# Moving the second pair's turn, the third pair's key loads and the sixth pair's loads in a fused attention and MLP kernel

## The chip, the cores and the metric

The kernel runs on one core of one Trainium2 chip. The metric is the device time of one execution in microseconds (us); lower is better. A core has a matrix engine (TensorE, in profiles PE, with its weight loads as PEld), a vector engine (VectorE, DVE), an activation engine (ScalarE, ACT), a general engine (GpSimd, POOL) and a sync engine (SyncE, SP) which here only issues DMAs. Each engine works through its own instructions in program order. Waits between engines go by semaphores. DMAs are issued by SP, ACT or POOL and run on 16 shared DMA engines.

## The reference

Attention with a threshold, over 8 batches of 8 heads with 576 rows of 64, then an MLP with exact GELU on the 4608 x 512 result.

```python
scores = scale * np.matmul(q, k.transpose(0, 1, 3, 2))
thresh = np.max(scores, axis=-1, keepdims=True) - tau
scores = np.where(scores >= thresh, scores, -1000000000.0)
scores = scores - np.max(scores, axis=-1, keepdims=True)
attn = np.exp(scores)
attn = attn / (np.sum(attn, axis=-1, keepdims=True) + 1e-09)
attn = np.matmul(attn, v).astype(np.float32)
...
h = x @ w_in                                            # 512 -> 2048
g = 0.5 * h * (1.0 + erf(h * inv_sqrt2))
return (g @ w_out).astype(np.float32)                   # 2048 -> 512
```

The MLP weights come in 64-bit floats, everything else in 32-bit floats.

## The kernel before

Heads are taken two at a time: a **pair** p holds two heads, 32 pairs in all, four to a batch. The 576 rows of a pair are four chunks of 128 and a tail of 64, so a pair has five pieces of work, one for each chunk i. One pass of the main loop is a **slot** (counted from 0): it computes the scores of one chunk of one pair on PE (`scores`, L366), their negated maxima on DVE (L378), thresholds on POOL (L379), exponentials on ACT (L381), and the thresholding with row sums on DVE (L397). Then DVE, POOL and ACT make two diagonal matrices of inverse sums (`diagonal`, L408, L411). In the next slot PE transposes the weights against these diagonals (`turn_p_early`, L308), and ACT copies them out of PSUM (L316, L320, L327). Later `weigh_v` multiplies them with the values (L483).

The first four pairs (p = 0 to 3) are the early ones. Their order is written out by hand: slots 0 to 7 take chunks 0 and 1 of pairs 0, 1, 2, 3 (slot 0 is pair 0 chunk 0, slot 1 is pair 0 chunk 1, slot 2 is pair 1 chunk 0, slot 4 is pair 2 chunk 0), slots 8 to 19 the other chunks of the four. `BATCH` is 20, the number of these slots. So slot 17 is chunk 2 of pair 3 and slot 18 its chunk 3.

`load_early` brings queries and keys of an early pair with rows on partitions: two DMAs for the main part and one for the tail, for queries (L248, L252) and for keys (L251, L252). `turn_qk_early` transposes both on PE (16 matmuls for queries, 16 for keys, L279; 8 small ones for the tails, L289), and copies them out of PSUM with five instructions: scaled queries on ACT (L282), keys (L284), two small copies of the key tail (L291, L292), and scaled query tails (two activations, L295). For pair 0 the key copies run on DVE, for the others on ACT. The pairs from 4 on are loaded by `load` in another layout, with runs of 128 bytes (L224 for q and k, L233 for v, after a small fill of the value tile by POOL, L228), and turned by DVE.

While the early pairs run, the weights are brought in 32 pieces of 512 columns, each by two DMAs (raw and shifted bytes, L155 and L157), and made 32-bit on DVE and ACT (L177, L178, L183, L185, L187). `load_piece` issues the next piece's DMAs once a piece has been used up: the first two from SP, the others from POOL. The buffers hold four pieces. `convert` places this work between the softmax steps of a slot. `fill` puts matmuls of the MLP (L558, L572) between the attention's wherever the weights are there. The last five blocks of 512 tokens are done after the attention with a scheme of seven products (L692).

The order of issue on each engine is that of the program. On SP it is: queries of pairs 0, 1, 2 (and what else `load_early` gives it), the first two weight pieces, values of pair 0, pair 3, values of pairs 1, 2, 3, then pair 4 and pair 5. SP has nothing else to do, so it comes to these long before the slot in whose text they stand, unless a buffer holds it up.

The piece of the main loop that the change touches:

```python
        if p < NP:
            scores(p, i)
            softmax_head(p, i)
            if p < HP - 1 and i == (1 if p == 0 else 0):
                turn_qk_early(p + 1)
```

Of the kernel before, what the change touches and what calls it, by code (L numbers as in the profile page):

```python
# [18 lines left out]
def kernel(  # L19
# [28 lines left out]
    nc = tc.nc  # L48
    ctx.enter_context(tc.manual_schedule())

    B, H, S, D = q.shape
    d_model, d_ff = moe_w_in.shape
    P = 128
    Q = 32
    HP = H // 2
# [4 lines left out]
    TAIL = S - MAIN  # L60
# [150 lines left out]
    def load(p):  # L211
        for _ in load_steps(p):
            pass
# [23 lines left out]
    def load_early(p):  # L237
        b, hp = divmod(p, HP)
        s = st[p] = {}
        for name, src in (("q", q), ("k", k)):  # L240

            pool, tag = (xg, "x") if p == 2 else (ld, name)
            t = s[name] = pool.tile([P, 2, NC + 1, D], FP32, tag=tag, name=name)
            eng = (nc.scalar, nc.gpsimd, nc.scalar)[p] if p < 3 and name == "k" else nc.sync
            for e in range(2):
                rows = src[b, 2 * hp + e, 0:MAIN, :]
                if name == "q":
                    eng.dma_start(t[:, e, 0:NC, :].rearrange("p (g c) d -> p g (c d)", c=2),  # L248
                                  rows.rearrange("(g p c) d -> p g (c d)", p=P, c=2))
                else:  # L250
                    eng.dma_start(t[:, e, 0:NC, :], rows.rearrange("(p t) d -> p t d", p=P))  # L251
            eng.dma_start(t[0:TAIL, :, NC, :], src[b, 2 * hp:2 * hp + 2, MAIN:S, :].rearrange("e s d -> s e d"))  # L252
# [8 lines left out]
    def turn_qk_early(p):  # L261


        s = st[p]
        if 2 <= p < HP:
            qT = op.tile([P, MAIN], FP32, tag="o_sb", name="qT")
            kT = pd_tail[p - 2].rearrange("p b i -> p (b i)")
        else:
            qT = ld.tile([P, MAIN], FP32, tag="qT", name="qT")
            kT = ld.tile([P, TAIL + S], FP32, tag="kT", name="kT")  # L270
        s["qT"], s["kT"] = qT, kT
        qt = s["q_tail"] = q_tail[p % 4]
        copy = nc.scalar.copy if p else nc.vector.tensor_copy
        for name in "qk":
            t = s[name]
            tr = ps.tile([P, NC, P], FP32, tag="mm", name="tr")
            for c in range(NC):
                for e in range(2):
                    nc.tensor.matmul(tr[e * D:(e + 1) * D, c, :], lhsT=t[:, e, c, :], rhs=ident, start=True, stop=True)  # L279
            src = tr.rearrange("p c s -> p (c s)")  # L280
            if name == "q":
                nc.scalar.activation(qT, src, AF.Copy, bias=0.0, scale=q_scale)  # L282
            else:
                copy(kT[:, TAIL:S], src)  # L284
        tr = ps.tile([P, NC, P], FP32, tag="mm", name="tr")
        for j, name in enumerate("qk"):
            t = s.pop(name)
            for e in range(2):
                nc.tensor.matmul(tr[e * D:(e + 1) * D, j, 0:TAIL], lhsT=t[0:TAIL, e, NC, :],  # L289
                                 rhs=ident[0:TAIL, 0:TAIL], start=True, stop=True)  # L290
        copy(kT[:, S:S + TAIL], tr[:, 1, 0:TAIL])  # L291
        copy(kT[D:P, 0:TAIL], tr[D:P, 1, 0:TAIL])  # L292
        for e in range(2):
            rows = slice(e * D, (e + 1) * D)
            nc.scalar.activation(  # L295
                qt[rows, e * TAIL:(e + 1) * TAIL], tr[rows, 0, 0:TAIL], AF.Copy, bias=0.0, scale=q_scale[rows])
# [60 lines left out]
    def scores(p, i):  # L357
        s = st[p]
        n = 1 if i == NC else 2
        sc = s["sc", i] = [ps.tile([P, 2, 512], FP32, tag="sc", name="sc", bufs=2) for _ in range(n)]  # L360
        for h in range(2):
            for e in range(n):
                rows = slice(0, P) if i == NC else slice(e * D, (e + 1) * D)
                lhsT = s["q_tail"] if i == NC else s["qT"][rows, i * P:(i + 1) * P]
                at = h * HALF + (TAIL if p < EARLY and e == 0 else 0)
                nc.tensor.matmul(  # L366
                    sc[e][:, h, 0:HALF], lhsT=lhsT, rhs=s["kT"][rows, at:at + HALF], start=True, stop=True)
# [150 lines left out]
    def gelus(left):  # L518


        while len(late) > left:
            g, j, hT = late.pop(0)
            t = gp.tile([P, 2, TOK], FP32, tag="g", name="g")
            if hold[0]:
                nc.scalar.copy(t, hT)
                held.append((g, j, t))
            else:
                gelu(g, j, t, hT)
# [6 lines left out]
    def gelus_held():  # L535
        hold[0] = False
        while held:
            g, j, t = held.pop(0)
            gelu(g, j, t, t)

    def table():

        if dirty[0]:
            nc.scalar.activation(warm[:, 1:2], warm[:, 0:1], AF.Exp)
            dirty[0] = False
# [274 lines left out]
    BATCH = HP * SLOTS  # L820
# [23 lines left out]
    for n in range(len(slots) + WEIGH + 1):  # L844
        p, i = slots[n] if n < len(slots) else divmod(n, SLOTS)
        early = p < EARLY
        last = slots[n - 1] if 0 < n <= len(slots) else None
        if p < NP:
            scores(p, i)
            softmax_head(p, i)  # L850
            if p < HP - 1 and i == (1 if p == 0 else 0):
                turn_qk_early(p + 1)
        elif n == len(slots):
            ext = weights_in()
        gelus(0)
        if n == BATCH:
            gelus_held()
        table()
        for args in due:
            weigh_v(*args)  # L860
        due = []
        if p > EARLY and i == WEIGH:
            for lo, hi in (0, WIDE), (WIDE, S):
                weigh_v(p - 1, lo, hi)
            if p == NP:
                divide(p - 1)
        owed += (goal(n) - goal(n - 1)) * BLK_NS * (PARTS[i] if not early and p < NP else 1.0)
        if early:
            fill(owed, tokens)
            owed = 0.0  # L870
            table()
        if last and last[0] < EARLY and last[1] < NC:
            turn_p_early(*last)
        if early and n > 2:
            convert(0, 700 if i == NC else 1)
        if p < NP:
            softmax_tail(p, i)
        if p < NP and not early:
            turn_p(p, i)
        if p < NP and not early:  # L880
            if i == 2:
                regroup(p, 1)
            if i > 2:
                regroup(p, i)
            if i == NC:
                divisors(p)
        if last and last[0] < EARLY and last[1] == NC:
            turn_p_early(*last)
        if p < 2 and i == 0:
            load_piece()  # L890
            load_v_early(p + 2)
        if p == 1 and i == NC:
            load(HP)
        if n == BATCH - 2:
            load(HP + 1)
        if n == BATCH:
            for t in pd_tail + [turned_p[:, e, h, :, :] for e in range(2) for h in range(2)]:
                nc.gpsimd.memset(t[:, NB:4 * KR, :], 0.0)
        if EARLY < p < NP and i == DIVIDE:
            divide(p - 1)  # L900
        if p >= HP and i == 1 and p + 2 < NP:
            loads = load_steps(p + 2)
        if p >= HP:
            next(loads, None)
        if p >= HP and i == 1 and p + 1 < NP or p == HP - 1 and i == 2:
            scale_q(p + 1)
        if p >= HP - 1 and i == 2 and p + 1 < NP:
            turn_qk(p + 1)
        convert(0 if n == 0 else 2000 if n < 3 else 3800 if n < BATCH - 1 else 1e9)
        if early:  # L910
            diagonal(p, i)
        if not early:
            lag[0] = 2 if p < NP else 0
            fill(owed, tokens)
            owed = 0.0
        if last and last[0] < EARLY:
            if last[1] == 1:
                due.append((last[0], 0, TOK))
            if last[1] == NC:
                due.append((last[0], TOK, S))  # L920
        if n == START - 1:
            tokens = TOK
        elif n == BATCH + 1:
            tokens = S
        elif p > EARLY and i == DIVIDE and p % HP == 0 or p == NP and i == WEIGH:
            tokens = p // HP * S
            leaving += [n for n in AWAY if n in x_blk and (n + 1) * TOK <= tokens]
        elif leaving and i < 2:
            put_away(leaving.pop(0))
# [34 lines left out]
```

## Time and profile before

| what | us |
|---|---|
| median of 7 runs | 1386.21 |
| lowest and highest run | 1385.11, 1387.45 |
| the profiled execution, whole | 1386.21 |
| its span, first to last instruction | 1384.4 |
| PE busy in the span | 1362.8 |

The profile shows one execution. An instruction has a start and a length; the time its engine stood idle before it is put down to what ended the wait. The chain of waits follows the work that ended last back from the end. A view by stretches gives the busy time of each engine between two times, the clock that was granted to PE (1.00 is full), the share of the DMA engines that was busy, and GB/s. In these rows the five numbers are PE, PEld, DVE, ACT and POOL.

The starts of the maxima (L378) mark the slots: 10.14 for slot 0, 14.79 for slot 1, 23.55 for slot 2, 29.09 for slot 3, 35.65 for slot 4. SP's own row at the start reads so:

```profile
4.54 1.11 SPq L248 DMA_DIRECT2D q<-in_q_dram  x2
7.20 0.60 SPq L252 DMA_DIRECT2D q<-in_q_dram  x1
7.92 0.52 SPq L155 DMA_DIRECT2D raw<-in_moe_w_in_dram  x1
```

These are the third pair's queries (pair 2), their tail, and the first weight piece.

### The profile page before, as it was taken

To read this page: it belongs to the slowest core of one execution; us is meant where nothing else is said; L and a number is where in the kernel's file an instruction comes from. 1 tells how busy PE (TensorE), PEld (TensorE's weight loads), DVE (VectorE), ACT (ScalarE), POOL (GpSimd) and SP (SyncE) were. 2 spreads that over 40 slices of the span, in tenths; PEclk is the share of its full clock that TensorE was granted. 3 is DMA by queue.
4 is the path that set the end of the run, shared out by engine and by line. 5 is a ranking of instruction groups with operands and counts; after the bars stand their busy time and mean duration, and the time that the engine had idled before them with its cause. 6 is when DMAs were issued, how large, how long until landed. Compare 5 with 4: busy or idle time off the path is not lost.

```text
span 1384.4 us, 20232 instructions
## 1 busy us (share of the span) xinstructions
PE 1362.8 (98%) x6734; PEld 970.4 (70%) x6734; DVE 893.2 (65%) x1742; ACT 638.2 (46%) x1158; POOL 435.9 (31%) x896
## 2 busy tenths in 40 slices
PE   8899999999999999999999999999999999999999
PEld 6676557466466466466476475588888888888887
DVE  6998777788888888878888888764142232241330
ACT  6766537457448358358367366241140230330420
POOL 4453344455555554554555551100000000000000
PEclk9999999999999999999999999999999999999999
DMA  8988376667777687687787775500000001001000
GB/s 264 322 298 241 68 162 144 144 156 179 154 174 177 156 193 172 156 206 167 160 206 169 163 187 121 113 0 8 23 1 23 23 1 46 16 0 54 9 8 23
DMA packets 215094, 169.19 MB, mean 122 GB/s; under 512 B 114176, under 2 KB 199488, under 8 KB 214992
## 3 DMA queue, kind: packets, MB, share of 16 engines
q1 hardware_dynamic: 190608, 112.54, 35.9%
q0 software_dynamic: 23520, 54.77, 13.4%
q8 instruction: 55, 0.90, 0.3%
q10 hardware_dynamic: 864, 0.59, 0.1%
q14 instruction: 47, 0.39, 0.1%
HBM read 72.73 MB, written 12.52 MB: 62 GB/s over the span
## 4 chain that ended last, share of the span: by engine, by line
PE 94%; DVE 2%; DMA 1%; ACT 1%; issue 0%; SPq 0%; POOL 0%; ACTq 0%; DVEq 0%
PE bank L692 35%; PE o_ps L572 17%; PE hT L558 16%; PE sc L366 13%; PE xT L483 11%; PE tr L308 2%; DVE p L397 1%; DVE nmx L378 0%; DMA k<-in_k_dram 0%; DMA turned_p<-in_moe_w_in_dram 0%; DVE power L185 0%; DMA x<-x 0%; ACT p L381 0%; DVE w_in L187 0%; PE tr L279 0%
## 5 line engine op out<-in xcount | busy, mean ns | idle before, releaser
L381 ACT ACTIVATE p<-sc,nmx 128x576 f32<-128x576 f32 x288 | 201.9, 737 | 269.9 <-DVE nmx L378 269.6
L397 DVE SCALAR_TENSOR_TENSOR p<-sc,thr,p 128x576 f32<-128x576 f32 x288 | 225.3, 815 | 61.4 <-ACT p L381 57.7
L378 DVE TENSOR_REDUCE nmx<-sc 128x1 f32<-128x576 f32 x288 | 205.5, 750 | 64.3 <-PE sc L366 63.4
L558 PE MATMUL hT<-x,w_in 128*128 128x256 f32 x1024 | 241.1, 385 | 0.0
L572 PE MATMUL o_ps<-w_out,g 128*128 128x512 f32 x512 | 237.8, 605 | 0.0
L558 PEld LDWEIGHTS hT<-x,w_in 128*128 128x128 f32 x1024 | 189.5, 190 | 49.2 <-issue 23.5
L379 POOL TENSOR_SCALAR thr<-nmx,tau_eff 128x1 f32<-128x1 f32 x288 | 89.0, 309 | 395.9 <-DVE nmx L378 395.5
L572 PEld LDWEIGHTS o_ps<-w_out,g 128*128 128x128 f32 x512 | 93.5, 191 | 111.2 <-issue 109.6
L483 PE MATMUL xT<-pT,v 128*64 128x256 f32 (+1 forms) x1280 | 163.9, 409 | 0.3 <-issue 0.3
L366 PE MATMUL sc<-kT,qT 64*128 64x288 f32 x960 | 157.4, 432 | 4.9 <-DVE p L397 4.1
L444 DVE STREAM_TRANSPOSE turned_p<-p 128x1152 f32<-128x1152 f32 x112 | 154.4, 1379 | 3.9
L366 PEld LDWEIGHTS sc<-kT,qT 64*128 64x128 f32 x960 | 89.4, 187 | 78.5 <-issue 67.1
L483 PEld LDWEIGHTS xT<-pT,v 128*64 128x64 f32 x1280 | 89.0, 137 | 72.6 <-issue 13.5
L692 PE MATMUL bank<-x,w_in 128*128 128x256 f32 x480 | 116.6, 379 | 0.0
L692 PE MATMUL bank<-w_out,unit 128*128 128x256 f32 x520 | 115.5, 379 | 0.0
L233 POOL DMA_DIRECT2D v<-in_v_dram x208 | 110.8, 536 | 4.5 <-issue 2.7
L692 PEld LDWEIGHTS bank<-w_out,unit 128*128 128x128 f32 x520 | 98.8, 190 | 13.4
L692 PEld LDWEIGHTS bank<-x,w_in 128*128 128x128 f32 x480 | 91.2, 190 | 12.8 <-issue 0.5
L692 PE MATMUL bank<-v,unit 128*128 128x256 f32 x320 | 82.1, 379 | 0.0
L224 POOL DMA_DIRECT2D q<-in_q_dram x104 | 70.8, 686 | 10.2 <-issue 8.9
L692 PE MATMUL bank<-unit,turned_p 128*128 128x256 f32 x320 | 73.1, 379 | 0.0
L531 ACT ACT_TABLE_LOAD x56 | 71.8, 1283 | 1.0
(163 smaller groups left out, 1492.6 us busy)
## 6 DMA issues: line engine op xcount, KB each, us to landing
pT<-turned_p SPq DMA_DIRECT2D x448, 160.0 KB, 3.6
pT<-pd_tail SPq DMA_DIRECT2D x112, 80.0 KB, 2.9
q<-in_q_dram POOLq DMA_DIRECT2D x104, 72.0 KB, 3.7
k<-in_k_dram POOLq DMA_DIRECT2D x104, 72.0 KB, 3.2
inv<-turned SPq DMA_DIRECT2D x56, 128.0 KB, 4.1
v<-in_v_dram POOLq DMA_DIRECT2D x156, 40.0 KB, 3.2
x<-x SPq DMA_DIRECT2D x10, 512.0 KB, 4.9
raw<-in_moe_w_out_dram POOLq DMA_DIRECT2D x8, 512.0 KB, 4.4
```

Of the source, the lines that this page charges most:

```text
L233: eng.dma_start(t[r:P:4, e, 0:n, :], rows[:, r * KR:r * KR + n, :])
L366: nc.tensor.matmul(sc[e][:, h, 0:HALF], lhsT=lhsT, rhs=s["kT"][rows, at:at + HALF], start=True, stop=True)
L378: nc.vector.tensor_reduce(nmx[:, e:e + 1], sc, axis=AXIS.XY, op=ALU.max, negate=True)
L379: nc.gpsimd.tensor_scalar(thr[:, e:e + 1], nmx[:, e:e + 1], -1.0, tau_eff, op0=ALU.mult, op1=ALU.subtract)
L381: nc.scalar.activation(w[:, e * S:(e + 1) * S].rearrange("p (h s) -> p h s", h=2), sc, AF.Exp, bias=nmx[:, e:e + 1], scale=1.0)
L397: nc.vector.scalar_tensor_tensor(row, sc[e][:, :, 0:HALF], thr[:, e:e + 1], row, op0=ALU.is_ge, op1=ALU.mult, accum_out=den[e])
L444: nc.vector.transpose(turned_p[:, :, i // 2, 0:NB, i % 2 * Q:(i % 2 + 1) * Q], w.rearrange("p (e b i) -> p e b i", e=2, i=Q))
L483: nc.tensor.matmul(to, lhsT=s["v"][:, e, c, :], rhs=rhs, start=(c == 0), stop=(c == KR - 1))
L531: nc.scalar.activation(t, src, AF.Gelu)
L558: nc.tensor.matmul(hT[:, j % 2, :], lhsT=w_in_sb[c][:, j * P:(j + 1) * P], rhs=x_blk[n][:, c, :], start=(c == 0), stop=(c == N_DM - 1))
L572: nc.tensor.matmul(o[:, 0:d_model], lhsT=g[j][:, m * P:(m + 1) * P], rhs=w_out_sb[j], start=(j == 0), stop=(j == N_DF - 1))
L692: nc.tensor.matmul(to, lhsT=l, rhs=r, start=start and k == 0, stop=k == len(pairs) - 1, skip_group_check=not start)
```

## The change

Four edits. The keys of pair 2 (the third) are issued by SP and no longer by ACT. The two small copies of the key tail run on ACT for pair 0 too. Pair 1 (the second) is turned in slot 0, behind the scores and the softmax head of slot 0, where it was turned in slot 1; pairs 2 and 3 keep their slots 2 and 4. `load(HP + 1)`, which brings pair 5 (the sixth), is called in slot 17 where it was called in slot 18.

```diff
@@ load_early @@
-            eng = (nc.scalar, nc.gpsimd, nc.scalar)[p] if p < 3 and name == "k" else nc.sync
+            eng = (nc.scalar, nc.gpsimd)[p] if p < 2 and name == "k" else nc.sync
@@ turn_qk_early @@
-        copy(kT[:, S:S + TAIL], tr[:, 1, 0:TAIL])
-        copy(kT[D:P, 0:TAIL], tr[D:P, 1, 0:TAIL])
+        nc.scalar.copy(kT[:, S:S + TAIL], tr[:, 1, 0:TAIL])
+        nc.scalar.copy(kT[D:P, 0:TAIL], tr[D:P, 1, 0:TAIL])
@@ main loop @@
-            if p < HP - 1 and i == (1 if p == 0 else 0):
+            if p < HP - 1 and i == 0:
                 turn_qk_early(p + 1)
...
-        if n == BATCH - 2:
+        if n == BATCH - 3:
             load(HP + 1)
```

## The prediction

> **What bounds the kernel now.** I read the page's engine totals first, then the stretches, then the chain of waits. TensorE (PE) sets the time:
>
> ```profile
> PE 1362.8 (98%) x6734; PEld 970.4 (70%) x6734; DVE 893.2 (65%) x1742; ACT 638.2 (46%) x1158; POOL 435.9 (31%) x896
> ```
>
> From 62.61 us on the chain is nearly all PE; behind it PE stands still for 2.37 us (130.37), 1.58 (160.95), 0.59 (617.83) and little else. Where the engines run the same order, whatever is gained before 62.61 us stays to the end. Before it PE waits and other engines lead. The chain of waits of the first slots (start, length, what):
>
> ```profile
> 4.58 3.52 DMA k<-in_k_dram
> 8.10 0.03 issue
> 8.13 0.70 ACT qT L282
> ...
> 12.75 0.72 PE sc L366 x2
> 13.47 0.01 issue
> 13.49 2.15 PE sc L366 x6
> 15.64 2.58 PE tr L279 x32
> 18.22 0.38 PE tr L289 x8
> ...
> 21.39 0.73 ACT power L178
> 22.12 0.02 issue
> 22.15 0.70 DVE power L185
> ```
>
> Two things are to be seen. The turn of the second pair (L279, L289) lies on the path in slot 1, 2.96 us of it. And PE stood idle just before, with the clock halved just after, as the timeline and the stretches (PE busy, ..., granted clock, DMA share, GB/s) show:
>
> ```profile
> 12.75 2.89 PE L366 MATMUL sc<-kT,qT 64*128 64x288 f32 x8 [2.56 <-DVE p L397]
> 22.15 0.69 DVE L185 SCALAR_TENSOR_TENSOR power<-raw,power 128x512 uint32<-128x512 uint32 x1 [3.00 <-ACT power L178]
> 62.61 1.65 PE L308 MATMUL tr<-diag,p 128*128 128x128 f32 x6 [3.23 <-ACT diag L411]
> ```
>
> ```profile
> 10.18:13.60 3.42, 0.84 (x5) 0.44 (x6) 2.94 (x6) 1.41 (x2) 0.77 (x3) 1.00 0.95 266
> 13.60:17.01 3.41, 3.41 (x20) 2.43 (x22) 2.25 (x4) 1.98 (x4) 1.82 (x5) 0.50 1.04 385
> 57.97:61.38 3.41, 1.41 (x12) 0.69 (x8) 3.10 (x9) 2.00 (x4) 2.48 (x5) 1.00 1.00 389
> 61.38:64.80 3.42, 2.19 (x10) 2.19 (x11) 3.42 (x8) 2.08 (x5) 0.81 (x3) 0.50 1.00 356
> 64.80:68.21 3.41, 3.41 (x18) 2.58 (x19) 2.98 (x8) 2.24 (x5) 1.62 (x3) 0.50 0.88 336
> ```
>
> From 22.15 to 62 us VectorE (DVE) leads: 29.45 of 30 us busy from 29 to 59. The DMA engines are as full (share 1.05); before that they are free for a moment:
>
> ```profile
> 26.00:29.00 3.00, 2.64 (x22) 1.87 (x22) 2.78 (x8) 2.94 (x9) 2.11 (x4) 1.00 0.38 102
> 29.00:59.00 30.00, 27.72 (x242) 20.51 (x240) 29.45 (x66) 24.71 (x54) 15.55 (x31) 1.00 1.05 299
> ```
>
> **Keys of the third pair, from ScalarE (ACT) to SP.** ACT issues them at 4.58 to 6.02 and 7.42 to 8.02, 2.04 us, and only then scales the first queries (8.13), which PE had turned by 6.92 (6.53 + 0.39). Freed, ACT does so at 6.95 to 7.64. The scores also need kT, which DVE copies from 7.83 to 8.52 as now, so they begin at 8.57 for 8.87: 0.30 us gained. The two small kT copies now on ACT cost 0.22 + 0.21 (its rows of the next pair) at 8.2 to 8.65, earlier than DVE's end at 8.90; nothing.
>
> On SP the three issues stand behind the third pair's query tail (7.20 to 7.80), so the first weight piece goes out at about 9.6 for 7.92, and all that SP issues after it (piece 1, values, fourth pair, fifth pair) 1.2 to 1.7 us later. Pieces 0 and 1 landed at 12.40, 14.74, 16.04 and 17.36 (raw, shifted, twice); plus 1.7 they are there at 14.1, 16.4, 17.7 and 19.1. DVE asks for them (see below) at 17.3, 18.0, 17.65 and 23.7: nothing lost, as ACT is what DVE waits for next. The keys land near 13 and are read at 18.9.
>
> **Turn of the second pair, to slot 0.** Its queries and keys landed by 8.32, so nothing holds it. I walk the new order with the durations of the rows. Scores of slot 0 end at 9.9; PE then turns: 16 query matmuls 1.1 (as at 22.05, full clock), 16 key matmuls 1.04, tails 0.6: to 12.7, inside the idle 2.56 us. Scores of slot 1 start at 12.7 for 12.75, need 1.24 as at 20.88 and end at 13.95 for 15.64. DVE takes its maxima from 13.65 for 14.79.
>
> ACT pays: exponentials of slot 0 to 12.04, then the five copies of the turn, 2.4 us, to 14.4. Behind them wait the two diagonals, ready at 13.6: 14.4 to 15.1 for 13.90 to 14.59, 0.5 us later than now; for them wait the transposes of slot 0's weights on PE. Exponentials of slot 1: 15.05 to 16.45 for 15.58 to 17.21; DVE's thresholding to 17.3 for 18.1. PE transposes slot 0's weights from 15.15 to 17.6 (2.42) for 18.52 to 20.94. ACT copies them (0.58, 0.58, 0.27) to 17.9 and starts L178 at 17.95 for 21.39. L185 follows at 18.7 for 22.15, L187 ends at 20.1, and the maxima of slot 2 start at **20.2 for 23.55: 3.35 us earlier**, the first 0.30 included. The step is 2.96 us of turn and about 1 us of halved scores, less what ACT adds.
>
> One rule of the Trainium skill speaks against the clock part. "TensorE: Matmul & The Clock Gate", Part 1, has the rate halve after an idle window of some 3.4 us. A gap of 2.56 us would then cost no clock, and the step were 2.3 to 2.5 us. The row shows 0.50 after a window with 0.84 us of PE work in it. I follow the row: 3.35.
>
> **What is late next.** The weights loop. DVE frees a piece's buffers, POOL issues the next, four are in flight. Piece 6 landed 0.02 us before its first use (41.06), piece 8 0.49, piece 11 0.02: DMA is as near the bound as DVE. High end: every issue and landing moves with DVE, 3.35 us. Low end, by room on the DMA engines: the hole at 26 to 29 closes (3 x 0.62 = 1.9 us, since piece 4, issued at 27.51, now goes out at 24.2), but the keys' load leaves a hole of about 1.4 us near 9 (their data, 1.0 us, moved behind the tail's issue), so 0.5. The fifth pair's slow loads (28.49 on; medians of 16.9 and 15.2 us to landing) start later and give some 0.5 back: 1.0. Between the ends no row decides; I take the middle, **2.2 us earlier at the end of this stage**, with DVE waiting about 1.1 us in all for pieces 5 to 11.
>
> **The halved clock at 61.38.** PE idles from 59.38 to 62.61, then runs at half rate to 68.21: (68.21 - 62.61)/2 = 2.8 us lost. With the gap 2.2 us earlier (57.2 to 60.4) and the windows where they are, one falls before full work again: 61.38 to 64.80 at half, 1.7 us lost, 1.1 gained. The halved stretches of this trace all start within 0.1 us of multiples of 3.413 us from its start. The same page says the window runs free of a kernel's start; then the gain averages nothing. One trace can't tell; I take half, 0.55.
>
> **Sixth pair's loads, slot 17.** SP has nothing between the two places; it issues q and k from 104.02 to 118.58 as now, since it only waits behind the fifth pair's values. Only the values move: they wait for POOL's fill of their tile (0.31 us at 133.73), which comes behind the row at 123.86, where POOL idles 3.46 us anyway. Eight DMAs go from 134.07 to about 124.4. They keep the DMA engines 1.3 us (their queue has 18.5% of the engines from 134 to 141) beside pieces 29 to 31, which land 2.96, 3.73 and 3.32 us before use. Nothing; without that cover, up to 1.3 us. Behind them on SP stands the regrouping of 156.23; it doesn't wait for them.
>
> **Sum.** 2.2 + 0.55 = 2.75 us. The profiled execution took 1386.21 (span 1384.4, 1.8 around it), which is also the median: 1386.2 - 2.75 = **1383.5**.
>
> **Rivals.**
> 1. Everything kept: the pieces come as early as DVE asks, and the windows help: 3.35 + 1.1 = 4.4, **1381.8**. For it: 350 to 400 GB/s were moved where the fifth pair's loads don't interfere. Against: DMA share 1.05 for 30 us.
> 2. DMA takes nearly all: 0.5 to 1.0 left, no clock gain, **1385.5**. For it: the slacks of 0.02. Against: the open hole at 26 to 29.
> 3. Slower: DVE's new waits for pieces open PE gaps between 30 and 60, and these bring halved windows that are not there now (a gap of 2.09 at 47.41 brings none, 1.64 us of PE work being in its window; one with 1.41 brings one). Each costs 1.7 us where PE has no room, and it was busy 27.7 of 30. One new window beside an advance of 2.2 leaves a gain; two turn the sign (+1.2); three give +2.9, **1389.1**.
>
> That the turn doesn't fit is excluded by the landings at 8.32.
>
> **Chances.** Forecast 54%, its own range 1382.0 to 1385.0; rival 1 20%, rival 2 16%, rival 3 10%. A difference of 0.2% (2.77 us) is about what a measurement can tell here, and the forecast sits on it: half of it, 27, counts as faster, 27 as same. Faster 0.27 + 0.20 = 0.47, same 0.27 + 0.16 = 0.43, slower 0.10. Range: rival 1 with a further half window (0.8) below, 1381.0; above, rival 2 with no gain and 0.5 for the loop, 1386.7.
>
> **What would show it.** Right: the turn's matmuls between 10 and 13, no halved window at 13.6, maxima of slot 2 near 20.2, DVE idle on DMA in L177 between 30 and 60 for 1 us or so, the transposes of 62.61 near 60.4. Wrong: maxima of slot 2 later than 21.5; DVE without DMA waits (rival 1), or over 2 us of them (rival 2); new windows at half clock between 20 and 58 (rival 3); a changed distance from the transposes of 62.61 to the end beyond the clock's part.

## The result and the profile after

The changed kernel takes 1381.94 us (median of 15 runs, 1379.08 to 1384.24), the kernel before 1386.22 (36 runs). The ratio is 0.9968, 95% interval 0.9961 to 0.9975: 4.4 us faster (3.5 to 5.4). The profiled execution took 1380.76 us with a span of 1378.7, 5.7 us below the span of before: the profiled pair lies further apart than the medians.

The stretches of the changed kernel that answer to those shown of before (PE busy first; the last three numbers are clock, DMA share, GB/s):

```profile
8.44:11.86 3.42, 3.28 (x48) 2.56 (x45) 2.66 (x5) 2.19 (x5) 0.60 (x2) 1.00 0.84 211
11.86:15.27 3.41, 3.25 (x22) 2.30 (x21) 2.40 (x6) 3.32 (x10) 2.00 (x5) 1.00 0.95 315
...
56.40:59.64 3.24, 0.03 (x2) 0.00 (x0) 2.58 (x6) 1.08 (x3) 1.50 (x3) 1.00 1.10 345
59.64:63.05 3.41, 3.32 (x15) 3.32 (x16) 3.41 (x9) 2.22 (x5) 1.04 (x3) 0.50 1.00 371
```

PE has no hole in slots 0 and 1 any more (3.28 and 3.25 us of work in 3.4), and the clock stays full there. The large gap ahead of slot 8's transposes is still there, with one halved window behind it for two before.

The timeline of the changed kernel, at the places shown of before:

```profile
11.59 1.94 PE L366 MATMUL sc<-kT,qT 64*128 64x288 f32 x8
17.39 0.43 DVE L177 TENSOR_SCALAR power<-turned_p 128x512 uint32<-128x512 uint32 x1 [0.71 <-DMA turned_p<-in_moe_w_in_dram]
18.16 0.68 DVE L185 SCALAR_TENSOR_TENSOR power<-raw,power 128x512 uint32<-128x512 uint32 x1
57.02 0.43 DVE L177 TENSOR_SCALAR power<-turned_p 128x512 uint32<-128x512 uint32 x1 [1.09 <-DMA turned_p<-in_moe_w_in_dram]
59.73 1.01 PE L308 MATMUL tr<-diag,p 128*128 128x128 f32 x3 [3.30 <-ACT diag L411]
```

L185 comes at 18.16 for 22.15, and DVE no longer waits for ACT in front of it. What waits now is L177, for a weight piece: 0.71 us at 17.39 and 1.09 at 57.02. The chain of waits of the changed kernel's first 20 us says where that piece comes from:

```profile
6.69 0.34 SPq L251
...
8.19 0.60 SPq L155
...
9.31 8.06 DMA turned_p<-in_moe_w_in_dram
17.37 0.02 issue
17.39 0.43 DVE power L177
```

Before, the chain ran through the turn on PE. Now it runs through SP: the third pair's keys (L251), the first piece's issue (L155), the second piece's DMA.

### The profile page after: what moved, and what is told of

The parts are those of the page before. It is cut to its first block, busy times and chain, and to the rows that moved or that the text cites. A ratio compares the mean times of both kernels' runs of the same rounds, so it can differ in the third digit from the quotient of the medians.

```text
span 1378.7 us, 20234 instructions
## 1 busy us (share of the span) xinstructions
PE 1360.2 (99%) x6734; PEld 968.0 (70%) x6734; DVE 892.8 (65%) x1740; ACT 638.0 (46%) x1160; POOL 435.1 (32%) x896
## 4 chain that ended last, share of the span: by engine, by line
PE 94%; DVE 2%; DMA 2%; ACT 1%; issue 0%; SPq 0%; POOL 0%; ACTq 0%; DVEq 0%; POOLq 0%
PE bank L692 35%; PE o_ps L572 17%; PE hT L558 16%; PE sc L366 13%; PE xT L483 11%; PE tr L308 2%; DMA turned_p<-in_moe_w_in_dram 1%; DVE p L397 0%; DVE power L185 0%; DVE nmx L378 0%; DMA k<-in_k_dram 0%; ACT p L381 0%; DVE w_in L187 0%; DVE power L177 0%; DVE w_in L183 0%
## 5 line engine op out<-in xcount | busy, mean ns | idle before, releaser
L692 PEld LDWEIGHTS bank<-w_out,unit 128*128 128x128 f32 x520 | 98.8, 190 | 13.4
```

The lines of the kernel that those rows point to most:

```text
L692: nc.tensor.matmul(to, lhsT=l, rhs=r, start=start and k == 0, stop=k == len(pairs) - 1, skip_group_check=not start)
```

## The experiments

Times are always beside runs of the kernel before on the same chip. "The changed kernel" is the one predicted.

### Which of the edits brings it

**The turn alone**, twice:

```diff
-            if p < HP - 1 and i == (1 if p == 0 else 0):
+            if p < HP - 1 and i == 0:
```

> The kernel before with one edit: the second pair is turned in slot 0. Theory (the turn fills the idle stretch of PE in slot 0 and that is the gain): 3 to 4 us below the kernel before, ratio about 0.9975, maxima of slot 2 near 20.5 us for 23.55. Rival (freeing ACT of the key issues is what counts, and the turn pays only with it): at most 1.5 us below the kernel before, maxima of slot 2 later than 22.

> The turn alone once more. Theory: 3.3 to 4.2 us below the kernel before, ratio 0.9970 to 0.9976; maxima of slot 2 come 11 to 12 us after the first scores. Rival (the turn needs the freed ACT for the rest): 2.5 us below or less, ratio above 0.9982.

Measured: 1381.95 us, ratio 0.9976 (0.9967 to 0.9986), then 1382.39 us, 0.9974 (0.9964 to 0.9985). That is 3.3 and 3.6 us. The maxima of slot 2 come at 19.09 and 20.02, both 11.2 us behind the first scores. The turn's matmuls and these maxima in the first of the two profiles:

```profile
9.12 1.09 PE L279 MATMUL tr<-ident,q 128*64 128x128 f32 x16
...
19.09 1.40 DVE L378 TENSOR_REDUCE nmx<-sc 128x1 f32<-128x576 f32 x2
```

The theory holds: the turn needs no other edit.

**The keys alone** (`(nc.scalar, nc.gpsimd)[p] if p < 2` in the kernel before), and the changed kernel with **the turn alone put back**, which leaves keys, tail copies and loads:

> The kernel before with one edit: the third pair's keys are issued by SP. Theory (the turn is the gain): 0.3 to 0.8 us below the kernel before, ratio 0.9994 to 0.9998; the first scores start 0.3 us earlier, pieces of weights land 1 to 1.5 us later and nobody waits for them. Rival (the keys count): 1.5 us or more below the kernel before, ratio below 0.9990.

> The changed kernel with the turn alone put back into slot 1; keys on SP and loads in slot 17 stay. Theory (the turn is the gain, some 3.7 us, the rest 0.5 or less): 0 to 1 us below the kernel before, ratio 0.9993 to 1.0000; maxima of slot 2 come 14.5 to 16 us after the first scores. Rival (keys and loads bring a part that shows only together): 1.5 us or more below, ratio below 0.9989.

Measured: 1384.62 us, ratio 1.0001 (0.9990 to 1.0011), and 1385.92 us, 1.0002 (0.9991 to 1.0012). Neither edit group shows a gain. An effect of 0.5 us lies inside both intervals, so the 0.3 to 0.8 expected of the keys alone is neither shown nor excluded; the rivals' 1.5 us is excluded in both. The hole and the halved clock are back, as the stretches of the kernel with the turn put back show:

```profile
8.86:12.27 3.41, 0.82 (x6) 0.32 (x3) 2.73 (x5) 1.40 (x2) 0.60 (x2) 1.00 0.78 197
12.27:15.68 3.41, 3.41 (x16) 2.03 (x16) 1.89 (x6) 1.43 (x3) 1.71 (x4) 0.50 0.97 323
```

**The sixth pair's loads back in slot 18**, all else changed (`if n == BATCH - 2:`):

> The changed kernel with the sixth pair's loads back in slot 18. Theory (they are hidden in either place): as the changed kernel, 4.0 to 4.6 us below the kernel before, ratio 0.9967 to 0.9971. Rival (the move brings part of the gain, by the stretch of 127 to 134 us which is 1.5 us shorter in the changed kernel): 2.5 to 3 us below the kernel before, ratio 0.9979 to 0.9982, and the slot after 126 us is longer.

Measured: 1379.93 us, ratio 0.9963 (0.9951 to 0.9975), the same as the changed kernel within the intervals. The loads are hidden in either slot. The rival is refuted at its stretch too: slot 18 lasts 7.6 us here as in the changed kernel, for 9.1 before. What goes with that difference is the clock, below.

### The weight loop and the fifth pair's loads

The changed kernel with the fifth and sixth pair's loads issued by POOL:

```diff
-        eng = nc.sync if p < HP + 2 else nc.gpsimd
+        eng = nc.gpsimd
```

> The changed kernel with the fifth and sixth pair's loads issued by POOL in their slots 13 and 17, where SP issues them as early as 28 us. Theory (their short packets slow the weight pieces between 28 and 58 us): DVE's wait of 1.09 us for a piece at 57 us goes, the transposes that stand at 59.7 us start about 1 us earlier, and the kernel is 1 us or more below the changed kernel (ratio to before 0.9960 or less) if POOL's added issues, sixteen in each of two slots, cost nothing. Rival (the DMA engines are full with the weights alone): the wait stays, and POOL's issues delay weight pieces in slots 13 and 17: 0 to 5 us above the changed kernel.

Measured: 1395.31 us, ratio 1.0072 (1.0059 to 1.0086). The time refutes the theory, and it is worse than the rival's 5 us. Between 30 and 100 us DVE waits for no piece any more, as the theory had it; slot 8's maxima come 38.2 us after slot 2's, for a mean of 39.5 in the eight profiles with the turn in slot 0 and the loads early on SP. That fits loads which slow the pieces, but it is one profile, and single ones with the loads on SP come down to 38.4 (before) and 38.6 (turn alone). The price on POOL is larger than either side expected. Timeline of this kernel, POOL and DVE:

```profile
93.13 2.75 POOL L224 DMA_DIRECT2D q<-in_q_dram  x4
95.87 2.63 POOL L224 DMA_DIRECT2D k<-in_k_dram  x4
...
104.52 0.59 POOL L379 TENSOR_SCALAR thr<-nmx,tau_eff 128x1 f32<-128x1 f32 x2
104.88 0.82 DVE L397 SCALAR_TENSOR_TENSOR p<-sc,thr,p 128x576 f32<-128x576 f32 x1 [7.52 <-POOL thr L379]
```

Sixteen issues keep POOL from 93.13 to 103.39, the thresholds stand behind them, and DVE waits 7.52 us. The sixth pair's issues, from 128.43 on, do the same once more: at 141.57 DVE has waited 5.56 us for POOL's thresholds. The two waits come close to the 13.4 us by which this kernel lies above the changed one.

The changed kernel with the fifth pair's queries and keys kept on SP but **held back to slot 8**:

```diff
+            if p == HP:
+                nc.gpsimd.memset(t[:, 0, 0:1], 0.0)
...
+        if n == 8:
+            fifth = load_steps(HP)
+            next(fifth)
+            next(fifth)
         if p == 1 and i == NC:
-            load(HP)
+            for _ in fifth:
+                pass
```

> The changed kernel with the fifth pair's queries and keys held back until slot 8, by a small fill of their tiles on POOL, and still issued by SP. Theory (their short packets slow the weight pieces from 28 to 58 us): DVE's waits for pieces between 30 and 58 us go, the transposes that stood at 59.7 us start near 58, as where POOL issued the loads, and the kernel is 1 to 3 us below the changed kernel, since pieces from slot 8 on come 2 to 4 us before use. Rival (the loads only move their price): waits of 1 us or more at pieces between 62 and 100 us, and the time of the changed kernel within 0.7 us.

Measured: 1381.87 us, ratio 0.9973 (0.9963 to 0.9982); the rival. SP issues the loads at 62.69. Between 30 and 60 DVE waits for no piece, but then it does, as its timeline shows:

```profile
75.30 0.43 DVE L177 TENSOR_SCALAR power<-raw 128x512 uint32<-128x512 uint32 x1 [0.91 <-DMA raw<-in_moe_w_out_dram]
78.43 0.43 DVE L177 TENSOR_SCALAR power<-turned_p 128x512 uint32<-128x512 uint32 x1 [1.04 <-DMA turned_p<-in_moe_w_out_dram]
```

Nor did slot 8's transposes come near 58: they start at 59.51, since slot 3 took 7.9 us here for 6.5 (PE and ACT stood there; why was not followed up). DVE's waits for pieces in the first 130 us sum to 3.8 us, for 3.6 in the first profile of the changed kernel: the waits moved, they did not go.

### The halved clock

Each kernel once more, the one before for its profile alone:

> The changed kernel once more, beside the others of this call. Theory (the halved clock windows lie anew in each execution, and a PE gap halves the clock where it falls inside one window): ratio to before 0.996 to 0.998, and the profile's halved stretches stand elsewhere against the same gaps than in the first one. Rival (the windows are fixed against the kernel's start): the same stretches at 46.0, 59.6 and 158.6 us.

> The kernel before once more, for its profile. Theory (windows free of the start): the first full clock comes at another time than 6.77 us, and the stretch after the gap of 130 us is halved only if the gap lies inside one window; the slot that took 9.1 us there takes 7.6 if it is not. Rival (fixed windows): halved at 13.6, 61.4 and 133.1 us again.

The changed kernel: 1380.96 us, ratio 0.9967 (0.9954 to 0.9979). Full clock comes first at 5.54 us there and at 5.03 in its first profile; in the two of before at 5.37 and 6.77. So the windows are not fixed against the start, and the theory holds on that. Its other half hardly came true: in the two profiles of the changed kernel the windows lie only 0.5 us apart, and the same three gaps have a halved window behind them (from 46.50, 60.16 and 159.14 for 45.98, 59.64 and 158.62). Nor are the windows shown to be wholly free of the start: in all fourteen profiles the first full clock comes between 4.72 and 6.77 us, in thirteen between 4.72 and 6.01, while windows without any tie to the start would spread over 3.41 us. In the second profile of before (its one run took 1388.81 us) slot 18 took 9.0 us, its gap again within one window. The gap ahead of slot 18's transposes shows what the windows do. Two pairs of windows, first the changed kernel again, then the turn alone:

```profile
124.98:128.39 3.41, 1.52 (x8) 0.98 (x6) 3.37 (x7) 2.34 (x6) 0.70 (x2) 1.00 0.86 323
128.39:131.80 3.41, 3.09 (x23) 2.69 (x24) 3.13 (x9) 2.25 (x7) 0.34 (x1) 1.00 0.08 27
```

```profile
124.88:128.29 3.41, 1.04 (x7) 0.64 (x6) 3.41 (x10) 2.87 (x7) 0.70 (x2) 1.00 0.56 225
128.29:131.71 3.42, 3.42 (x19) 2.87 (x17) 2.28 (x5) 1.17 (x2) 0.65 (x2) 0.50 0.12 27
```

Almost the same gap, but in the first one a window's edge cuts it (1.52 us of PE work left in the window), and in the second it lies in one window (1.04). Over all profiles that have this gap, but the one with loads on POOL (2.28 of its 2.31 us in one window, halved) and the one with loads held back (1.73 in one window, not halved):

| profile | gap, us | its part in one window | halved after | slot 18, us |
|---|---|---|---|---|
| before, before again, turn alone, idle matmuls | 2.37 | 2.37 | yes | 9.0 to 9.2 |
| turn alone again | 2.20 | 2.20 | yes | 9.1 |
| changed again | 2.21 | 1.93 | no | 7.6 |
| loads back | 2.06 | 1.63 | no | 7.6 |
| changed | 1.81 | 1.48 | no | 7.6 |
| keys alone | 2.13 | 1.24 | no | 7.6 |
| turn put back | 1.68 | 1.09 | no | 7.6 |

It is not the gap's length: 2.20 us was followed by a halved window and 2.21 was not. Slots with a halved window behind the gap are 1.4 to 1.6 us longer. Whether it is chance that it comes is open. All four profiles with the third pair's keys on ACT have it, of those with the keys on SP in this table only the one with idle matmuls; slots 17 and 18 together take 18.5 to 19.0 us in the former and 16.5 to 17.0 in the other five. A share of the keys in this was not tested. There isn't one threshold for every place: the gap of 1.58 us near 160 was followed by a halved window in all ten of these profiles, with 1.25 to 1.58 us of it in one window.

A profile shows one execution, but every run has its mean granted clock on record. A halved window of 3.41 us takes about 0.0012 off it (half of 3.41 in 1384). The mean is 0.9939 over the 75 runs of before that stand beside the experiments, 0.9955 over 20 runs of the turn alone, 0.9956 over 21 of the changed kernel, and 0.9935 over 22 of the two with keys on SP and the turn in slot 1. So the turn, with or without the other edits, takes away some 1.3 halved windows per execution. Among the 75 runs of before, one halved window more goes with 1.1 us more (a fit, give or take 0.1). By this estimate some 1.4 us of the gain come by the clock, the rest by the turn's own time.

The changed kernel with **24 idle matmuls** in slot 8's gap:

```diff
+            if n == 8:
+                fillt = ps.tile([P, 512], FP32, tag="mm", name="fillt")
+                for _ in range(24):
+                    nc.tensor.matmul(fillt[:, 0:P], lhsT=ident, rhs=ident, start=True, stop=True)
             turn_p_early(*last)
```

> The changed kernel with 24 idle matmuls (128 x 128, 2.9 us) on PE in slot 8, ahead of the transposes that wait at 56.4 to 59.7 us; their result is not used. Theory (the gap halves the clock behind it): no halved stretch begins between 58 and 66 us, and the kernel is 1 to 2 us below the changed kernel. Rival (the clock there costs nothing, since DVE leads): within 0.5 us of the changed kernel, or above it by what the matmuls hold up.

Measured: 1381.93 us, ratio 0.9972 (0.9961 to 0.9983), as the changed kernel. No window is halved between 5.72 and 128.59 us. But the matmuls took 5.62 us for the planned 2.9 (a 32-bit matmul shows as two rows in the profile, 24 as 48; I had counted rows, and the 16, 16 and 8 matmuls of a turn given above are rows too, 8, 8 and 4 matmuls), and slot 8's transposes start only at 60.32. The mean clock of its seven runs is 0.9971, about one halved window fewer than the changed kernel's, without a gain in time. The excess of the matmuls may have taken it; this run doesn't price the clock in slot 8.

**Real work in the gaps**, the changed kernel with a raised debt of `fill` in slot 18, and in slots 18 and 22:

```diff
+        owed += {18: 2400.0, 22: 1600.0}.get(n, 0.0)
         if early:
             fill(owed, tokens)
```

> The changed kernel with 2.4 us more of the MLP's matmuls given to slot 18 (the debt of fill is raised by 2400 ns there), taken from later slots; same work. Theory (PE's gap of 1.8 to 2.4 us ahead of that slot's transposes is idle time on the path, and halves the clock behind it in those executions in which it lies inside one window): 2 to 4 us below the changed kernel, ratio to before 0.9945 to 0.9955. Rival (the gap only moves, since DVE sets slots 17 to 19): within 1 us of the changed kernel, ratio 0.9960 to 0.9975, and the gap appears before the next slots.

> As the one with more matmuls in slot 18, and 1.6 us more of them in slot 22, where PE waits 1.58 us for DVE's thresholding ahead of the scores and the clock was halved behind it in nearly every profile. Theory (idle PE is lost time here too): another 1.6 to 3 us below that one, ratio to before 0.9925 to 0.9945. Rival (the gap moves to the following slots): no further gain.

Measured: 1382.20 us, ratio 0.9969 (0.9959 to 0.9980), and 1380.19 us, 0.9960 (0.9946 to 0.9975). The first is the rival: its gap in slot 18 is gone, and two others are there that were not. Timeline of that kernel:

```profile
144.91 3.70 PE L572 MATMUL o_ps<-w_out,g 128*128 128x512 f32 x8 [1.32 <-ACT g L531]
890.24 1.10 PE L692 MATMUL bank<-x,w_in 128*128 128x256 f32 x4 [1.89 <-DVE x L660]
```

The work taken ahead is missing later: at the change from hidden layer to output, and at the end of the attention, where PE now waits for DVE's sums. The second has its slot 22 gap gone, no halved window after 62.85, and has 2.08 us of idle PE at 885 in turn. It has the lowest ratio of all, but the intervals overlap with that of the changed kernel, so a gain over it is not shown.

## Why the prediction was right, and where its sizes were off

**The turn into slot 0: right, and larger than said.** The walk had the maxima of slot 2 at 20.2; the profile has 19.55, the first scores having come at 7.73 and not at 8.57. From the first scores to these maxima the four profiles with the turn in slot 1 take 14.7, 15.9, 14.7 and 16.0 us (mean 15.3), the eight with it in slot 0 and the loads early on SP 11.2 to 11.8 (mean 11.3). So the step is 4.0 us in the mean; the walk had 14.7 and 11.6, 3.05. The changed side is nearly as walked; the side of before was read from an execution with one halved window behind the hole, and where it took 15.9 and 16.0 there were two. That speaks for the clock's part: one more halved window went with 1.2 to 1.4 us more. The rule weighed there (the Trainium skill, "TensorE: Matmul & The Clock Gate", Part 1: the clock halves after an idle window of some 3.4 us) would have left only 2.3 to 2.5 us of this term. The measurement goes against it: the hole of 2.3 to 2.7 us was followed by a halved window in all four, and without the hole there was none before 45 us.

**The keys to SP: the start right in kind, the price missed.** First scores come at 7.9 in the mean of eight profiles with keys on SP, at 8.5 in four with keys on ACT: 0.6 gained for 0.3 said. Single ones overlap (7.7 to 8.1 against 7.9 to 8.9), and in the pair read here a part is the clock: PE turned the first pair's queries in 1.70 us for 2.43, the full clock coming at 5.03 for 6.77. But "nothing lost" on SP was wrong. The second piece landed at 17.37 and DVE stood 0.71 us for it (0.40 in the second profile), since it asked at 16.7 and not at 17.65 as walked. SP fell further behind than the 1.2 to 1.7 us said. The fifth pair's first issue came at 28.49 and 29.67 before, at 30.56 and 31.60 with keys on SP and the turn in slot 1, at 29.54 and 33.38 with the turn alone, and at 37.47 with both. The traces show what SP waits for, beside buffers: in this program the DMAs of SP and ACT report their landings on eight semaphores in turn, shared by both engines, and an issue waits until the DMA eight before it has landed. In the kernel before, the issue at 14.76 followed such a landing at 14.74; in no profile does either engine begin an issue with more than seven of their DMAs still to land. So SP's later issues go by landings, while the prediction added up the length of SP's own issues. Waits of DVE for pieces sum to 1.1 us in the mean of the four profiles with keys on ACT, to 2.9 of the eight with keys on SP; single ones go from 0.2 to 5.3, so this is a tendency. It fits that the two kernels with keys on SP and the turn in slot 1 gain nothing in time; that the waits are the reason was not isolated.

**What DMA takes back: the term that was most mis-sized.** The sum kept 2.2 of 3.35 us to the end of the weight loop. In the pair of profiles it looks right by chance: slot 8's transposes came 2.88 us earlier (59.73 for 62.61), of 4.0 gained at slot 2, so 1.1 went. But the kernel before has the same waits in other executions (1.81 us in its second profile, 0.54 in the one I read). From slot 2's maxima to slot 8's, profiles with the turn in slot 1 take 40.1 us in the mean, those with it in slot 0 39.5. So no loss to DMA is shown, where the sum had 1.15 us of it. The two means rest on four and eight profiles that range from 38.4 to 41.7 us and from 38.6 to 40.6, and the four include two with keys on SP: with keys on ACT it is 39.2 without the turn and 39.6 with it, with keys on SP 41.0 and 39.5. A loss of some tenths is not excluded. The slack of 0.02 us at three pieces was read as a limit that holds only the changed kernel; it holds both. The pair's other 2.8 us, of 5.7 between the spans, came behind slot 8, where the changed kernel's profile has two halved windows to 170 us for four.

**The halved clock at 61.38: a gain put in without ground.** On the windows the same page, "TensorE: Matmul & The Clock Gate", Part 1, says that they run free of a kernel's start, and these runs agree so far that they are not fixed against it (4.7 to 6.8 us to the first full clock). Behind slot 8's gap there were 2, 0, 2 and 2 halved windows with the turn in slot 1, and 1, 1, 0, 0, 1, 2 and 1 with it in slot 0 (the idle matmuls and the moved loads left out). One sign named for rival 3 did come: eight of the ten profiles with the turn in slot 0 have a halved window that opens between 45 and 47 us, where the profile read before had none. It did not make the stretch from slot 2 to slot 8 longer. By the mean clocks the windows outside the hole about cancel: 1.3 fewer per execution, where the hole alone had 1.5 behind it in the mean of four profiles.

**The sixth pair's loads: right.** 0.9963 without the move, 0.9968 and 0.9967 with it.

So rival 1, everything kept at 1381.8, is what the median of 1381.94 fits, but that its sum comes so close is luck: the maxima of slot 2 come 4.4 us earlier in the mean of two profiles each, for its 3.35, and its 1.1 us for the clock at 61.38 are not shown. The likeliest case had the mechanism. It had the step at slot 2 too small, and it charged 1.15 us for DMA where no loss is shown. The changed kernel gains 4.4 and 4.6 us, with the sixth pair's loads back 5.1, the turn alone 3.3 and 3.6; the intervals overlap, so whether the keys add a part beside the turn stays open.

## What to carry to other kernels

Work that stands on the path of one slot may be free in the slot before, if its engine has a hole there and its inputs are in: here a turn that took 2.96 us in slot 1, in part at half clock, takes 2.3 us in a hole of 2.6, and moving it gave 3.3 to 3.6 us, as the hole also had a halved clock behind it. Before a resource that is nearly full is charged with eating a gain, look at a second profile of the kernel before: if it waits there as well, the wait is no cost of the change. Where transfers fill the DMA engines over a long stretch, putting one later moved its price here, and putting it on a computing engine added the issue time to what stood behind it. And before an issue is moved to another queue, see what that queue waits for: here it was the landing of the DMA eight before.

## What the runs showed of the hardware that was not expected

- Whether a PE gap was followed by a halved clock hung on how a window of 3.41 us cut it: at one place 2.20 to 2.37 us inside one window were each time, 1.93 or less of a gap of up to 2.21 weren't. At another place 1.25 us in one window was enough.
- The windows lie differently in each execution, and the times carry it: 75 runs of the kernel before span 1381.17 to 1388.58 us, and one halved window more goes with 1.1 us more.
